# Another order of the units in all sixteen groups of a two-branch attention kernel

## The chip, the cores and the metric

One core of a Trainium2 chip runs the whole program. The metric is the device time of one execution in microseconds; the kernel before takes 842.63 us, the median of three runs from 841.31 to 843.46.

## The reference

The program computes two attentions over the same 2048 x 512 input `x` and mixes them by a gate per row.

```python
g = sigmoid((x * gate_w).sum(-1, keepdims=True))
a = A(x, mem0, Wq, Wk, Wv, Wo)      # recurrent, segment by segment
b = B(x, wq, wk, wv, wo, beta)      # four blocks of 512 rows
return g * a + (1 - g) * b

# A, for each of 64 segments of 32 rows:
h = concatenate([mem, xs])                   # 8 rows of memory, 32 of x
q, k, v = h @ Wq, h @ Wk, h @ Wv             # 32 heads of 128
p = softmax(where(mask, q @ k.T * scale, -1e9))
o = (p @ v) @ Wo
mem = o[:8]; outs.append(o[8:])
```

The eight rows of memory tie the segments together: segment s+1 can project nothing of its memory rows before segment s has ended its output projection. B is softmax attention inside blocks of 512 rows with 32 heads of 16, plus a linear memory that is summed over the earlier blocks.

## The kernel before, in words

**Stages.** First a stage projects the first three blocks of B and turns x (`b_projections`), while the weights of A (Wk, Wq, Wv of 4 MB each) arrive; at about 50 us `plan_a` begins, which is the rest of the program. It walks through 16 groups of four segments. All matrices stay on the chip.

**The recurrent trick.** In a segment, the kernel projects 32 rows: the 8 of memory and the first 24 of the segment. The last 8 rows of the four segments of a group do not depend on the memory for their projection, so they are projected for all four at once, one group ahead, as the *left* units (`KL`, `QL`, `VL`). Their attention output is kept and its output projection is made once a group too (`ol`, then `of`).

**Units.** `plan_a` does not issue its work in a fixed loop. Each piece is a *unit* with a short name, and each group has a list of names (`A_LIST0` to `A_LIST15`, lines 1045 to 1254) that is walked from left to right; a unit issues its instructions when its name comes up. Each engine then runs its instructions in the order in which they were issued, and semaphores hold an instruction until its operands are there. So the lists set the order on every engine and on the DMA queue of SP. `0.` to `3.` ahead of a name is the segment of the group, the digit behind it the half (b) of 16 heads:

- `Q0x`, `Q0y` (and `K`, `V`): the two halves of a projection, eight matmuls of 512 columns each (L1291); small `q0`, `k0`, `v0`: its copy out of PSUM; `TQ0`, `TK0`: the transpose on VectorE (L1303).
- `S`: scores (L1571, L1576); `X`: exponential on ScalarE (L1585); `Y`: mask on VectorE; `M`: sums by matmul (L1606); `L`: logarithm and exponential, the reciprocal of the sums, on ScalarE (L1613, L1616); `N`: normalisation on VectorE (L1620); `n`: the same for the left keys on POOL (L1626).
- `PV` (L1636) and `PL` (L1648): P times V for the segment's keys and for the left ones; `E0a`, ...: their copies out of PSUM; `W0a`, ...: a quarter of the output projection (L1378).
- `H0`, `H1`: the copy of the summed output (tile `WF`); `F0`, `F1`: the *fold*, a matmul that adds four partial sums (L1396); `hm`: the memory for the next segment; `ax`: the finished rows; `xc`, `qt`, `xl`, `oL`: copies on POOL.
- `bS`: scores of two steps of B (L919); `bE`: one exponential of B (L940) and, on a diagonal, the select on POOL (L946); `bP`: P times V of B (L972); `bT`: one of the small works behind it; `pj`, `pp`: projection and copy for the fourth block of B (L823).
- `wl`: issues a load of 512 KB of Wo, eight in all (L549). `VLt`: reloads the left V from DRAM, where the second `VL` copy stored it (L1326, L1334).
- `os`: turns a finished group's rows with one VectorE transpose and stores them with four DMAs (L1453, L1457). `tl`: loads such rows; `tb`, `tbe`, `tf`, `tfe`: the tail that multiplies B's output by its weights, mixes it with A's and stores it.

An `e` at the end of a left, `ol` or tail unit means its second part, mostly the copy out of PSUM. An `i` or a `p` ahead of a left unit belongs to the first or the last group. A name that has nothing to do is passed over.

**The mark `~`.** `A_ENG` says which engine makes a PSUM copy. A `~` behind a name swaps ScalarE and VectorE for that one:

```python
for u in ORDERS[g]:
    v.swap = u[-1] == "~"
    u = u.rstrip("~")
```

**Banks.** PSUM has eight banks. A unit takes its bank when it is issued and gives it back when its copy is issued; where none is free, `relief` issues a pending copy or an exponential of B ahead of its turn in the list. B's scores take two neighbouring pairs.

Of the kernel before, what the change touches and what calls it, by code (L numbers as in the profile page):

```python
# [854 lines left out]
class BAttn:  # L855
# [198 lines left out]
    2.S1 bE bT 2.V0y bE bE 2.X1 2.L0 2.n0 2.Y1 pj 2.v0~ 3.qt pj 2.M1 2.L1 2.N0 2.v1 bP 2.PV0 2.PL0 2.E0b 2.E0a~ pj 2.n1 2.N1 pj 2.PV1 2.PL1 bT pp 2.W0b
    2.E1b 2.W0a 2.E1a 2.W1b pp 2.W1a bP 2.H0 2.H1 bS 2.F0 2.hm0 2.F1 2.hm1~ 2.oL 3.K0x 3.K0y 3.xc 3.k0~ bE 2.ax1 bE bE 3.Q0x 3.Q0y bE 3.TK0 2.ax0~ 3.q0~
    3.Q1x 3.Q1y 3.TQ0 3.q1 3.TQ1 3.K1x 3.K1y 3.k1~ 3.S0 3.X0 3.Y0 3.V0x 3.V1x 3.V0y 3.M0 3.L0 3.n0 bP 3.TK1 3.S1 3.X1 3.V1y 3.v1~ 3.v0 3.N0 bP 3.Y1 3.PV0
    3.PL0 3.E0a~ 3.M1 3.L1 3.n1 pj 3.E0b~ pj 3.W0a 3.N1 3.PV1 pp 3.PL1 3.E1a~ 3.E1b~ 3.W0b 3.W1b 3.oL 3.W1a bS 3.H0 bE 3.F0 3.hm0 3.H1~ 3.ax0 bE 3.F1
# [3 lines left out]
    0.K0x 0.Q0x bE bE 0.Q0y 0.K0y 0.q0~ 0.TQ0 xl 0.k0 0.TK0 0.Q1x 0.K1x 0.Q1y 0.q1 bP bP 0.qt bT 0.K1y 0.k1 0.TK1 0.V1x 0.S0 0.X0 0.TQ1 0.V1y bS VL0x 0.Y0
    VL0 VL0e bE KL1x KL1 KL1e 0.M0 bE bE 0.V0x 0.V0y bE 0.v1~ 0.L0 0.S1 1.qt 0.N0 0.X1 0.Y1 0.n0 QL1x QL1 QL1e pj 0.M1 1.xc 0.v0~ 0.L1 0.n1 bP pj 0.PV0 pp
    0.PL0 0.E0a 0.E0b~ QL0x QL0 0.N1 0.PV1 0.PL1 0.W0b 0.E1a~ 0.W0a 0.W1a 0.E1b 0.W1b 0.H0 QL0e~ 0.H1~ VL1x VL1 0.F0 0.hm0 bP bS 0.xc 1.K1x VL1e 0.F1
    0.hm1~ 0.ax0 1.Q0x bE 1.K0x 1.K0y bE bE 0.ax1 1.k0~ 1.TK0 VLt 1.Q0y bE 1.q0~ 1.TQ0 1.K1y 1.k1 1.TK1 1.Q1x 1.Q1y bP 1.S0 bP 0.oL bS 1.V1x 1.V1y 1.q1
    1.TQ1 1.S1 1.X0 bE 1.V0x 1.Y0 1.M0 bT 1.V0y pj bE bE 1.X1 1.Y1 1.v0 1.M1 bE 1.L0 1.N0 1.n0 1.L1 pj 1.N1 1.v1~ KL0x 1.PV0 1.PL0 1.E0a 2.xc KL0 bP
    1.E0b~ bP 1.PV1 bT 1.n1 pp 1.PL1 1.E1b~ 1.E1a~ 1.W0b 1.oL KL0e~ 1.W0a 1.W1a 1.W1b 1.H0 bS pj 1.F0 1.H1 1.F1 1.hm1~ pj bE 1.hm0 2.K0x 1.ax0~ 2.K0y bE
    bE 2.Q0x 2.Q0y 2.K1x 2.K1y 2.Q1x bE 2.k0 2.TK0 pp bP bP 2.Q1y 1.ax1~ 2.q0~ 2.TQ0 2.q1 2.k1~ bS 2.qt 2.S0 2.V0x ol0x bE 2.TK1 2.X0 2.TQ1 2.Y0 bE 2.S1
    2.X1 2.Y1 2.V0y bE 2.M0 ol0 2.L0 2.n0 bE 2.V1x 2.M1 2.L1 2.n1 2.V1y 2.v0 2.N0 ol1x 2.v1 3.xc 2.PV0 2.PL0 2.E0b 2.N1 ol1 3.qt ol1e~ bP 2.E0a~ 2.PV1
    2.PL1 2.E1b 2.E1a 2.oL 2.W0b 2.W0a 2.W1a bP 2.W1b bS bT pj 2.H0 2.F0 2.H1 2.F1 2.hm1~ pj bE 2.hm0 3.Q0x 3.Q0y bE 2.ax1~ pp 3.K0x 3.K0y bE 3.Q1x 3.Q1y
    2.ax0~ bE 3.q0~ 3.TQ0 3.k0 3.TK0 3.K1x 3.K1y 3.S0 3.k1 bP 3.q1~ 3.V0x 3.TQ1 3.TK1 3.V0y 3.S1 bP 3.X0 3.X1 3.Y0 3.M0 3.L0 3.n0 3.V1x 3.V1y 3.v0 3.Y1  # L1070
    3.M1 3.N0 3.PV0 3.L1 3.n1 3.v1 3.N1 3.PL0 3.E0a 3.PV1 3.PL1 3.W0a 3.E0b 3.W0b 3.E1b 3.W1b 3.E1a~ 3.W1a 3.oL of ofe bS 3.H0 3.F0 3.H1 3.hm0 3.ax0 3.F1
# [4 lines left out]
    bE 0.V1x bT bE bE bE 0.V1y 1.xc 0.S1 0.X1 KL1x VL0x 0.Y1 0.X0 0.Y0 VL0 0.M1 0.M0 QL1x QL1 0.v0~ 0.v1 VL0e 0.L0 0.N0 0.n0 0.L1 0.n1 0.N1 KL1 0.PV0
    0.PL0 0.E0b~ QL1e~ bP bP QL0x 0.E0a 0.PV1 0.PL1 0.W0a 0.E1a~ 0.W0b 0.W1a KL1e~ 0.E1b~ 0.oL 0.W1b 0.H0~ 0.H1~ bS 1.qt bE QL0 0.F0 0.hm0~ 0.F1 VL1x
    0.ax0~ bE 1.K0x 0.hm1~ QL0e~ 1.Q1x 1.Q1y 1.q1~ 1.TQ1 bE bE 1.K0y 1.k0~ 0.ax1 1.Q0x 1.Q0y 1.TK0 1.q0~ 1.K1x 1.K1y bP bP bS 1.k1 1.TQ0 1.TK1 1.V0x 1.S0
    bE bE 1.X0 1.V0y 1.V1x 1.Y0 bE 1.v0 1.S1 2.qt 1.X1 1.Y1 1.V1y 1.v1 1.M0 1.L0 1.N0 1.n0 VL1 1.M1 1.L1 1.n1 KL0x bE 1.N1 1.PV0 1.PL0 1.E0a~ 1.E0b KL0
    KL0e~ 2.xc 1.PV1 1.PL1 1.E1a 1.E1b~ 1.W0b 1.W0a 1.W1a VL1e~ 1.W1b 1.H0 bP 1.H1 bS bP bT 1.F0 1.hm0 1.F1 1.hm1 2.K0x VLt 2.K0y 1.ax1 2.k0~ bE bE 2.Q0x  # L1080
    1.ax0 2.TK0 2.Q0y 2.K1x 2.K1y 2.Q1x 2.Q1y bE 2.q0 2.TQ0 bE 2.k1 2.TK1 1.oL 2.S0 bP bP 2.X0 bS ol0x ol0 bE 2.q1~ 2.TQ1 2.S1 3.qt 2.V0x 2.V0y bE 2.Y0 bE
    2.M0 2.X1 ol1x bE 2.Y1 2.L0 2.n0 2.M1 2.v0 2.L1 2.V1x 2.V1y 2.v1~ 2.n1 2.N0 2.PV0 2.PL0 bP bP 2.N1 ol1 2.E0b~ 2.E0a 2.PV1 2.PL1 2.E1a 2.W0b 2.E1b~
    2.W0a bT 2.W1a ol1e bT 2.W1b 2.H0 bS of 2.F0 bE 2.hm0 3.xc 2.ax0 2.H1~ 2.F1 2.hm1~ 2.ax1~ 3.K0x ofe~ bE 3.Q0x 3.Q0y 3.q0 3.K0y bE 3.k0 3.TK0 3.TQ0 bE
# [776 lines left out]
```

## Time and profile before

| | |
|---|---|
| time, median of 3 runs | 842.63 us (841.31 to 843.46) |
| the profiled execution's own time | 841.9 us |
| its span, first to last instruction | 839.7 us |
| TensorE (PE) busy | 806.0 us, 96% |
| ScalarE (ACT) busy | 590.3 us, 70% |
| VectorE (DVE) busy | 576.5 us, 69% |
| POOL busy | 286.1 us, 34% |
| granted TensorE clock | 1.00 |
| DMA | 57.48 MB, most of it in the first 80 us |

How to read it: busy time of TensorE counts a matmul from its start to its modelled end, and matmuls overlap in the pipeline, so two that follow at once and two with a short gap between can both look busy. The distance from start to start tells more than the busy share. "Idle before" a group is time in which its engine stood, with the engine and line whose work ended that time.

### The profile page before, as it was taken

Reading aid. Unit: us, or ns where it says so; the run is one execution under the profiler, and the core shown is the slowest. Engines: PE = TensorE matmul, PEld = TensorE weight load, DVE = VectorE, ACT = ScalarE, POOL = GpSimd, SP = SyncE. Lnnn points to the kernel's source line nnn. Section 1 sums busy time; section 2 is a strip of 40 time slices with the busy share of each in tenths; the row PEclk is TensorE's granted clock in tenths of the full one; section 3 lists DMA queues with packets and bytes.
Section 4 is the critical chain, followed back from the end, with each engine's and each line's share of the span. In section 5 each row is a group of like instructions: output and inputs, shape, how many; then the busy total and the mean of one; then the engine's idle time right before and its main releaser. Section 6 shows DMA issues by size and latency. Waiting matters only on the chain.

```text
span 839.7 us, 49011 instructions
## 1 busy us (share of the span) xinstructions
PE 806.0 (96%) x21927; PEld 431.3 (51%) x21933; DVE 576.5 (69%) x1395; ACT 590.3 (70%) x1506; POOL 286.1 (34%) x780
## 2 busy tenths in 40 slices
...
PEclk9999999999999999999999999999999999999999
...
GB/s 324 418 360 228 67 45 60 48 31 54 25 30 40 31 44 34 44 38 46 25 44 39 24 56 25 47 38 46 37 19 55 22 55 26 47 35 16 29 41 46
DMA packets 98225, 57.48 MB, mean 68 GB/s; under 512 B 71768, under 2 KB 92128, under 8 KB 96480
## 3 DMA queue, kind: packets, MB, share of 16 engines
...
## 4 chain that ended last, share of the span: by engine, by line
PE 84%; ACT 6%; DMA 4%; DVE 3%; issue 1%; SPq 1%; DVEq 0%; ACTq 0%
PE ps L1291 45%; PE ps L1378 17%; PE ps L1396 3%; PE ps L1636 3%; PE ps L919 2%; PE ps L686 2%; PE ps L972 2%; DMA scr_mzd<-MZ 2%; PE ps L1571 2%; PE ps L1487 1%; PE ps L1606 1%; ACT PT L940 1%; ACT R_sb L1616 1%; ACT WF L390 1%; PE ps L704 1%
## 5 line engine op out<-in xcount | busy, mean ns | idle before, releaser
L946 POOL TENSOR_SCALAR_AFFINE_SELECT PT<-PT 128x128 bf16<-128x128 bf16 (+2 forms) x320 | 118.1, 369 | 202.4 <-ACT PT L940 155.5
L940 ACT ACTIVATE PT<-ps 128x512 bf16<-128x512 f32 x320 | 175.1, 610 | 5.7 <-PE ps L919 4.6
L1291 PE MATMUL ps<-Wv_sb,hT 128*32 128x512 bf16 x2048 | 138.4, 379 | 0.0
L1291 PE MATMUL ps<-Wq_sb,hT 128*32 128x512 bf16 x2048 | 136.7, 379 | 0.7
L1291 PE MATMUL ps<-Wk_sb,hT 128*32 128x512 bf16 x2048 | 135.9, 379 | 1.4 <-ACT PT L940 1.1
L1378 PE MATMUL ps<-Wo_sb,OT_sb 128*32 128x512 bf16 x2048 | 129.2, 380 | 0.7 <-ACT OT_sb L390 0.6
L1626 POOL TENSOR_TENSOR P_sb<-P_sb,R_sb 128x64 bf16<-128x64 bf16 x128 | 51.0, 398 | 135.6 <-ACT R_sb L1616 129.4
L390 ACT ACTIVATE OT_sb<-ps 128x320 bf16<-128x320 f32 x170 | 68.7, 435 | 23.4 <-PE ps L1648 21.9
L1291 PEld LDWEIGHTS ps<-Wk_sb,hT 128*32 128x32 bf16 x2048 | 58.0, 97 | 47.6 <-ACT hT L390 2.1
L1291 PEld LDWEIGHTS ps<-Wq_sb,hT 128*32 128x32 bf16 x2048 | 57.7, 97 | 48.0 <-ACT hT L390 3.6
L390 ACT ACTIVATE WF<-ps 128x256 f32<-128x256 f32 x105 | 35.2, 382 | 55.2 <-PE ps L1378 53.0
L1378 PEld LDWEIGHTS ps<-Wo_sb,OT_sb 128*32 128x32 bf16 x2048 | 47.9, 96 | 45.4 <-ACT OT_sb L390 7.3
L1303 DVE STREAM_TRANSPOSE QT_sb<-QN_sb 128x256 f32<-128x256 f32 x128 | 56.3, 440 | 21.6 <-ACT QN_sb L390 18.0
L390 ACT ACTIVATE QN_sb<-ps 128x512 bf16<-128x512 f32 x78 | 46.9, 604 | 34.3 <-PE ps L1291 32.8
L1303 DVE STREAM_TRANSPOSE KT_sb<-KN_sb 128x256 f32<-128x256 f32 x128 | 56.3, 440 | 20.8 <-ACT KN_sb L390 17.7
L390 ACT ACTIVATE KN_sb<-ps 128x512 bf16<-128x512 f32 x75 | 45.1, 602 | 31.8 <-PE ps L1291 31.1
L1585 ACT ACTIVATE P_sb<-ps 128x224 bf16<-128x224 f32 x128 | 45.9, 360 | 28.4 <-PE ps L1576 20.3
L1291 PEld LDWEIGHTS ps<-Wv_sb,hT 128*32 128x32 bf16 x2048 | 50.1, 95 | 24.3 <-ACT aT_st L390 0.6
L1620 DVE TENSOR_TENSOR P_sb<-P_sb,R_sb 128x160 bf16<-128x160 bf16 x128 | 42.2, 330 | 20.2 <-ACT R_sb L1616 18.2
L392 DVE CAST V_sb<-ps 128x512 bf16<-128x512 f32 x76 | 51.8, 682 | 5.4 <-PE ps L1291 4.8
L392 DVE CAST OT_sb<-ps 128x320 bf16<-128x320 f32 x86 | 41.1, 486 | 19.0 <-PE ps L1648 18.1
L1636 PEld LDWEIGHTS ps<-P_sb,V_sb 32*128 32x128 bf16 x2048 | 23.3, 91 | 59.7 <-DVE P_sb L1620 25.2
...
## 6 DMA issues: line engine op xcount, KB each, us to landing
...
```

What stands on the lines that cost most here:

```text
L390: P.op("act", lambda a: a.activation(dst, src, ACT.Copy), reads=[v.rbank[k] for k in bks], writes=dres, name=name)
L392: P.op("dve", lambda d: d.tensor_copy(dst, src), reads=[v.rbank[k] for k in bks], writes=dres, name=name)
L940: P.op("act", lambda a: a.activation(pt, v.pb[bk], ACT.Exp, scale=v.SCALE_B), reads=[v.rbank[bk]], writes=[rp], name="be%d_%d" % (n, t))
L946: P.op("gp", lambda g: g.affine_select(mv, mv, [[0, len(cut)], [1, 128]], ALU.is_ge, 0.0, base=0, channel_multiplier=-1), reads=[rp], writ ...
L1291: ins = pe.matmul(pb[bk][SEG * j:SEG * (j + 1), :], lhs(c), cols(w, j) if split else w[:, 512 * j:512 * (j + 1)], start=(c == 0), stop=(c ...
L1303: P.op("dve", lambda d: d.transpose(to, src), reads=reads, writes=writes, name=name)
L1378: ins = pe.matmul(pb[bk][SEG * j:SEG * (j + 1), :], lhs(4 * k + j), Wo_sb[:, 4 * k + j, :], start=(first and k == ks[0]), stop=False, skip ...
L1396: ins = pe.matmul(pb[bk][SEG * j:SEG * (j + 1), SEG * n:SEG * (n + 1)], cols, v.fold[:, :], start=True, stop=True, skip_group_check=True)
L1585: P.op("act", lambda a: a.activation(P_sb[:, b, :], pb[bk][:, 0:224], ACT.Exp, scale=SCALE), reads=[rbank[bk]], writes=[Rs("P%d" % b), Rs( ...
L1620: P.op("dve", lambda d: d.tensor_tensor(wide(P_sb, b)[:, :, 0:L], wide(P_sb, b)[:, :, 0:L], R_sb[:, b, :].rearrange("p (i q) -> p i q", q= ...
L1626: P.op(ENG["n"], lambda d: d.tensor_tensor(left(P_sb), left(P_sb), grp04(R_sb[:, b, :]), ALU.mult), reads=[Rs("R%d" % b)], writes=[Rs("P%d ...
L1636: ins = pe.matmul(pb[bks[j]][:, L * i:L * (i + 1)], V_sb[SEG * j:SEG * (j + 1), b, i * E:(i + 1) * E], P_sb[SEG * j:SEG * (j + 1), b, LW * ...
```

## The change

All sixteen lists are replaced by others with the same units. Nothing else of the program differs: the same functions, tiles, engines by default (`A_ENG`) and DMA transfers. In some lists the number of `bE`, `bP`, `bT`, `os`, `tf` and `tfe` differs by one to five, and other lists make up for it. The marks `~` stand at other units, so that 13 PSUM copies in the balance go from VectorE to ScalarE (1506 and 1519 instructions on ScalarE, 1395 and 1382 on VectorE). TensorE has the same instructions in another order, POOL and SP too. The unit `os`, the turn by VectorE, stands at other places: within the first eleven units of a group mostly before, and in groups 8, 13 and 15 some 40 to 50 units in now.

The beginning of the first list, and a stretch of the second half of the last:

```diff
 A_LIST0 = """
-    ixl iKL0x iQL0x iQL0 iQL1x iQL1 iKL0 pj iKL1x iKL0e iKL1 wl 0.Q1x 0.Q1y iQL1e pj 0.K0x 0.K0y 0.q1 0.TQ1 iQL0e~ iKL1e~ bS wl bE iVL0x 0.V0x bE 0.V0y bE
-    0.xc bE 0.Q0x 0.v0~ pp 0.Q0y 0.q0 0.TQ0 bS bP wl bP 0.qt 0.k0~ 0.TK0 pj bE pj wl bE 0.S0 0.X0 iVL0 iVL1x iVL1 0.K1x wl 0.K1y iVL0e~ bE 0.Y0 0.M0 pj xl
-    pp 0.k1 iVL1e wl wl iVLt bE 0.L0 0.TK1 bP wl 0.S1 0.X1 bS 0.Y1 bP bE bE pj bE KL0x 0.M1 0.n0 bE 0.L1 pp 0.V1x 0.V1y 1.xc QL0x 0.v1 QL0 QL0e~ QL1x QL1
-    bP 0.N1 VL0x VL0 0.N0 QL1e~ bT 0.n1 KL1x KL1 VL1x VL0e bP KL0 VL1 KL1e~ 0.PV0 0.PL0 pj VL1e~ 0.E0b~ 0.E0a 0.PV1 0.PL1 0.E1a~ 0.E1b~ KL0e 0.W0a 0.W0b
-    bS pj bE VLt bE bE 0.W1a 0.W1b 0.H0 0.F0 0.oL 0.H1 0.F1 0.hm1~ 1.qt 0.hm0 pp 1.Q1x 1.Q1y 1.Q0x 1.Q0y bE 1.q0 1.TQ0 1.K0x 1.q1 1.TQ1 1.K0y 1.k0 1.TK0
...
+    wl ixl iQL0x iKL0x 0.Q1x 0.Q1y iKL0 iKL0e~ wl iQL0 iQL0e~ 0.Q0x 0.Q0y iQL1x iQL1 0.K0x 0.K0y 0.k0 iQL1e pj 0.q1 wl iKL1x iKL1 iKL1e~ bS bE 0.V0x 0.q0
+    iVL0x 0.TQ0 0.V0y 0.V1x pj 0.V1y iVL0 0.TK0 pj pp 0.v1 bE 0.qt bE iVL0e~ pj bE iVL1x iVL1 xl bS iVL1e bP 0.xc bP QL0x bE bE 0.TQ1 0.v0 0.S0 wl 0.K1x
+    0.K1y KL1x bE wl 0.X0 0.Y0 bE KL1 pj pp 0.k1~ KL1e wl iVLt wl 0.TK1 0.M0 0.L0 QL0 bP wl QL0e bS 0.N0 bP bE VL0x VL0 0.S1 1.qt bE 0.X1 bE QL1x 0.Y1
+    VL0e QL1 pj pp QL1e~ 0.M1 0.L1 KL0x KL0 0.n0 0.n1 VL1x VL1 bE 0.PV0 0.PL0 0.N1 pj 0.E0a 0.E0b~ KL0e 0.PV1 0.PL1 0.E1b~ 0.E1a VL1e~ pj VLt 0.W0b 0.W0a
+    bP 0.W1a bP pp bT 0.W1b 0.H0 0.H1~ 1.xc bS 0.F0 bE 0.hm0 0.ax0 0.F1 0.hm1~ 1.K0x 0.oL bE 1.Q0x 1.K0y 1.k0~ 1.Q1x 1.Q1y 1.q1~ bE 1.TK0 1.Q0y bE 1.K1x
...
 A_LIST15 = """
...
-    2.v0 2.L1 2.n1 tb 2.N1 2.M0 of 2.PV1 2.PL1 2.L0 2.n0 2.E1a ofe 2.N0 2.PV0 2.E1b 2.PL0 2.E0a~ 2.W1a 2.W1b tbe 2.W0a 2.E0b 2.oL 2.W0b 2.H0 2.H1~ os pl0x
-    tf 2.F0 2.hm0 2.ax0 pl0 2.F1 2.hm1 3.K0x 3.Q1x 3.K0y 3.Q0x tfe 3.Q0y 3.K1x 3.K1y 3.k0 tl 3.Q1y 3.TK0 3.q0 3.TQ0 3.k1 3.TK1 pl1x 3.S0 3.V0x 3.q1 3.V0y
...
+    tbe tfe tl 1.E0a 1.E0b 1.PV1 1.n1 1.PL1 1.E1b 2.xc 1.W0a 1.W0b 1.E1a~ 1.oL 1.W1b 1.W1a of ofe os 1.H0 1.H1 1.F0 1.hm0 1.ax0 1.F1 1.hm1 2.qt 1.ax1~
...
+    2.V0x 2.V0y 2.v1 2.Y0 2.n1 2.M0 2.N1 2.PV1 2.v0~ 2.L0 2.PL1 2.E1a 2.E1b tb 2.N0 2.PV0 2.n0 2.PL0 2.E0b 2.W1a tbe tf 2.W1b 2.W0b 2.E0a~ 2.W0a 2.oL pl0x
+    2.H0 2.H1 2.F0 2.hm0 pl0 2.F1 2.hm1 3.K0x tfe 3.Q0x 2.ax0~ 3.Q0y 3.q0~ 3.K0y 3.k0 3.TQ0 3.K1x 3.K1y 3.Q1x tl 3.Q1y 3.TK0 3.S0 3.V0x 3.k1~ 3.q1 3.TK1
...
```

341 lines of the change are left out of this document (170 added, 171 removed).

## The prediction

> **What bounds the kernel now.** First the page: its engine rows, the granted clock, the chain that ended last.
>
> ```profile
> span 839.7 us, 49011 instructions
> PE 806.0 (96%) x21927; PEld 431.3 (51%) x21933; DVE 576.5 (69%) x1395; ACT 590.3 (70%) x1506; POOL 286.1 (34%) x780
> PEclk9999999999999999999999999999999999999999
> PE 84%; ACT 6%; DMA 4%; DVE 3%; issue 1%; SPq 1%; DVEq 0%; ACTq 0%
> ```
>
> TensorE is busy 96% of the span at full clock, but the chain that ended last passes through it for only 84%. The other 16%, some 134 us, is time in which TensorE's next work hung on somebody else, though its pipeline still showed older matmuls as busy. Only that part can move: the change keeps every TensorE operation. Next, where it lies by stage: columns are the window, its length, and busy time (instructions) of PE, weight loads, DVE, ACT, POOL, then clock, DMA share and GB/s.
>
> ```profile
> 54.50:81.30 26.80, 22.45 (x524) 10.37 (x520) 15.45 (x34) 17.56 (x38) 8.38 (x23) 1.00 0.84 262
> 116.80:788.50 671.70, 656.81 (x18788) 353.91 (x18787) 485.15 (x1182) 495.09 (x1290) 238.32 (x610) 1.00 0.16 38
> 788.50:839.70 51.20, 43.76 (x1264) 22.48 (x1264) 30.67 (x75) 24.72 (x67) 7.36 (x19) 1.00 0.17 42
> ```
>
> The first segment (54.5 to 81.3) has TensorE idle for 4.4 us in 27, with the DMA engines 84% busy. Groups 1 to 14 idle only 15 us in 672, the last group 7 in 51. Then the two matmul groups that wait most, P times V (L1636) and the fold (L1396); after the bar stand busy time, mean duration and idle time before them.
>
> ```profile
> L1636 PE MATMUL ps<-P_sb,V_sb 32*128 32x40 bf16 x2048 | 35.5, 177 | 13.4 <-DVE P_sb L1620 7.6 <-ACT OT_sb L390 2.9 <-ACT V_sb L390 0.4
> L1396 PE MATMUL ps<-fold,WF 128*32 128x32 f32 x2048 | 36.9, 199 | 5.3 <-ACT WF L390 2.6 <-ACT hT L390 0.7 <-DVE oTt L996 0.2
> ```
>
> They hold 18.7 us of TensorE's 33.7 idle. A stretch of one segment in the middle, TensorE alone in order of time (start, duration):
>
> ```profile
> 467.37 0.60 PE L1291 MATMUL ps<-Wk_sb,hT 128*32 128x512 bf16 x8
> 467.80 0.60 PE L1291 MATMUL ps<-Wq_sb,hT 128*32 128x512 bf16 x8
> ...
> 471.99 0.28 PE L1606 MATMUL ps<-P_sb,onesb 128*32 128x160 bf16 x8
> 472.09 1.06 PE L1291 MATMUL ps<-Wv_sb,hT 128*32 128x512 bf16 x16
> 473.01 0.28 PE L1606 MATMUL ps<-P_sb,onesb 128*32 128x160 bf16 x8
> 473.12 0.28 PE L972 MATMUL ps<-PT,Vj 128*32 128x128 bf16 x8
> 473.63 0.27 PE L1636 MATMUL ps<-P_sb,V_sb 32*128 32x40 bf16 x16 [0.22 <-DVE P_sb L1620]
> 473.79 0.21 PE L1648 MATMUL ps<-P_sb,VL 32*128 32x64 bf16 x4
> 473.93 0.62 PE L1291 MATMUL ps<-Wv_sb,xL 128*32 128x512 bf16 x8
> 474.55 0.28 PE L1636 MATMUL ps<-P_sb,V_sb 32*128 32x40 bf16 x16
> ```
>
> A unit of eight 512-column matmuls costs 0.43 us (467.37 to 467.80), wherever it stands. After the sums (L1606) ScalarE takes logarithm and exponential, VectorE multiplies, and only then P times V can run: 471.99 to 473.63 and 473.01 to 474.55, so 1.5 to 1.6 us. What the list puts between is the cover; where it is shorter, TensorE stands. So the order of the units is the whole matter.
>
> **The change part by part.** The instructions of TensorE, POOL and the DMA queue are the same in number; sixteen lists are permuted, and the marks that swap a PSUM copy between ScalarE and VectorE are set anew, by which 13 copies go from VectorE to ScalarE.
>
> *Covers outside the first segment.* I counted in both lists, for each segment, the TensorE work (0.43 us per unit as above, the smaller units at their spacing in the same view) that stands between a producer and its consumer, and took as need the shortest distance at which the trace shows no wait: 1.4 us from sums to P times V, 0.63 from the last output projection to the fold, 0.37 from the fold to the next projection, 0.63 from P times V to the output projection, 1.36 from projection to scores, 1.0 from scores to sums. Missing cover, before and after: sums to P times V 21.6 and 20.0 us (47 and 48 places short of 128), output projection to fold 7.5 and 7.7, fold to projection 5.8 and 5.4, P times V to output projection 4.6 and 3.7, projection to scores 2.0 and 1.7, scores to sums 1.8 and 2.0. In all 43.3 and 40.5, so 2.8 us less, 1.05 of it in the first segment, which is costed by itself below: 1.75 us remain, from nine segments that get better by over 0.1 us and seven that get worse. The price of a missing microsecond: the two rows above waited 13.4 + 5.3 = 18.7 us for 21.6 + 7.5 = 29.1 missing, 0.64 each. That is -1.1 us; ends: -1.75 (price 1) and 0 (what the queues of ScalarE and VectorE add hides it).
>
> *The first segment.* Its waits in order:
>
> ```profile
> 56.95 0.40 PE L919 MATMUL ps<-QTj,KTj 32*128 32x256 bf16 x8
> 60.42 0.40 PE L919 MATMUL ps<-QTj,KTj 32*128 32x256 bf16 x8 [0.80 <-DVE QN_sb L392]
> 61.39 0.40 PE L972 MATMUL ps<-PT,Vj 128*32 128x256 bf16 x8 [0.57 <-ACT V_sb L390]
> 66.81 0.29 PE L972 MATMUL ps<-PT,Vj 128*32 128x256 bf16 x4 [1.02 <-POOL PT L946]
> 76.14 0.21 PE L1648 MATMUL ps<-P_sb,VL 32*128 32x64 bf16 x4 [0.90 <-DMA VL<-scr_vld]
> 80.62 0.61 PE L1396 MATMUL ps<-fold,WF 128*32 128x32 f32 x32 [0.55 <-ACT WF L390]
> ```
>
> The first two waits stand behind the second block of B's scores (`bS`). Between the first and second `bS` the old list has five units (`iVL0x 0.V0x 0.V0y 0.Q0x 0.Q0y`, 2.2 us), the new one eleven (4.7 us); the trace needed 3.5 (56.95 to 60.42). Both waits go: -1.4. The one thing that could bring them back is the copy of V, which stood until a store of the stage before had landed:
>
> ```profile
> 57.40 2.07 ACT L940 ACTIVATE PT<-ps 128x512 bf16<-128x512 f32 x4 [0.50 <-PE ps L919]
> 60.74 0.60 ACT L390 ACTIVATE V_sb<-ps 128x512 bf16<-128x512 f32 x1 [1.28 <-DMA scr_mzd<-MZ]
> ```
>
> With the new list the second `bS` comes at about 62, after that copy's 61.4. The third wait (1.02) is for B's four exponentials and POOL's select; ScalarE takes them at 0.52 us each (2.07 for four), and in the old order six other copies stood among them. The new one puts one exponential of A there: 0.33 + 4 x 0.52 + 0.36 + 0.37 of select, about 3.3 with the steps between, against 3.8 of list: -0.8.
>
> ```profile
> L1585 ACT ACTIVATE P_sb<-ps 128x224 bf16<-128x224 f32 x128 | 45.9, 360 | 28.4 <-PE ps L1576 20.3
> L946 POOL TENSOR_SCALAR_AFFINE_SELECT PT<-PT 128x128 bf16<-128x128 bf16 (+2 forms) x320 | 118.1, 369 | 202.4 <-ACT PT L940 155.5
> ```
>
> These rows give the 0.36 and 0.37. The fourth, for the left V's way through DRAM, hangs on SP and the weights of Wo:
>
> ```profile
> 57.63 1.05 SPq L549 DMA_DIRECT2D Wo_sb<-in_A_Wo_dram  x2
> ...
> 65.60 0.43 SPq L1326 DMA_DIRECT2D scr_vld<-VNL  x1
> 66.08 1.57 SPq L549 DMA_DIRECT2D Wo_sb<-in_A_Wo_dram  x2
> 71.68 2.65 SPq L1334 DMA_DIRECT2D VL<-scr_vld  x4
> ```
>
> The new list issues the store some 2.8 us earlier with three loads of 512 KB of Wo ahead instead of five, but TensorE also comes some 4 us earlier. At 262 GB/s (the window above) five to six loads take 10 to 11 us from 57.6; with 4.5 more for the reload (71.68 to 76.14) the data come at 71.7 to 73.5, wanted at 71.7: a wait of 0 to 1.8. I take 0.9, so no gain, and keep 0.9 either way. The fifth loses 0.3, since a `bS` of 0.33 now stands ahead of the fold. First segment: -2.5 us (ends -3.8 and 0).
>
> *Mode switches.* Work on 32-row tiles (P times V, `bS`) after work on 128-row tiles pays something even where nothing waits:
>
> ```profile
> 415.76 1.91 PE L1378 MATMUL ps<-Wo_sb,OT_sb 128*32 128x512 bf16 x32
> 417.60 0.40 PE L919 MATMUL ps<-QTj,KTj 32*128 32x128 bf16 x12
> ```
>
> Four units of 0.43 are 1.73, and the switch came after 1.84: 0.11. Such switches go from 201 to 203: +0.2 us.
>
> The Trainium skill, "TensorEngine Tiling (Array Packing)", section Key Properties, says that changing the tiling mode drains TensorE; the trace agrees, with 0.11 us. By the rule alone, two switches more, the change would be 0.2 us slower, and the sum has it.
>
> *The row turn `os`.* Fifteen times VectorE turns a group's rows, and SP issues four stores.
>
> ```profile
> L1453 DVE STREAM_TRANSPOSE aT_st<-aT_st 128x256 f32<-128x256 f32 x15 | 6.4, 429 | 0.0
> L1303 DVE STREAM_TRANSPOSE KT_sb<-KN_sb 128x256 f32<-128x256 f32 x128 | 56.3, 440 | 20.8 <-ACT KN_sb L390 17.7
> ```
>
> What it delays is the next operation on VectorE. In the old lists that is a copy or a turn of K or Q, on the way to scores, 10 times of 15; in the new ones 9 times, and two stand ahead of `norm` (groups 8 and 13). One fewer is a gain of 0.4 us at most, two in P times V's chain a loss of 0.9 at most; I take 0 and keep both ends. The tail's reload stays a group behind, so the stores cost nothing on SP.
>
> *The 13 copies,* fourteen of Q and K more and some others fewer:
>
> ```profile
> L390 ACT ACTIVATE QN_sb<-ps 128x512 bf16<-128x512 f32 x78 | 46.9, 604 | 34.3 <-PE ps L1291 32.8
> ```
>
> At 604 ns that is 7.8 us more on ScalarE, which is idle for 249 us (839.7 less 590.3): 0, but see the second rival.
>
> *Sum:* -1.1 - 2.5 + 0.2 = -3.4 us. The profiled execution took 841.9 (839.7 and 2.2 around it), which makes 838.5; the median shown is 842.63, 0.7 above it, so I predict 839.2.
>
> **The rivals.** *No change:* the weights set when the first segment ends, since the last piece of Wo must have landed before its last output projection, and TensorE merely waits later. Then -2.5 becomes 0: 842.6 - 1.1 + 0.2 = 841.7. For it: the DMA share of 0.84 there. Against: no output projection waited for Wo before, and Wo's issues now stand earlier.
>
> *Slower, ScalarE as local bound:* summing durations by list, ScalarE has more work than TensorE in 11 segments before (10.4 us over) and in 15 after (14.4 over), the worst being segments 2 and 51 with 2 us. If the surplus lands on P times V's chain, it costs 4.1 us once, or twice, 8.2, when both blocks' logarithms queue behind it. The middle, 6.1, less the first segment's 2.5: 846.2. It decides from the point where a segment's surplus is over what the next segment leaves free (1 to 2 us). Against: segments 29 and 30 of before, 0.8 and 2.3 over by their lists, have these windows, and in the second, the worst of all, TensorE did not idle at all; ScalarE showed 10.3 us of work in 12.7, since its instructions overlap in part.
>
> ```profile
> 419.10:430.60 11.50, 10.39 (x313) 6.03 (x309) 6.65 (x16) 9.17 (x26) 3.87 (x9) 1.00 0.12 31
> 430.60:443.30 12.70, 12.70 (x368) 6.58 (x361) 8.43 (x23) 10.28 (x27) 4.96 (x13) 1.00 0.25 62
> ```
>
> **How the numbers follow.** Forecast 0.50, no change 0.24, slower 0.26. A difference under 0.3% (2.5 us) is about what a measurement cannot tell. The forecast's own range: first segment -3.8 to 0, covers -1.75 to 0, turn -0.4 to 0.9, switches 0.2: 837 to 844. Taking in the slower case, and 3 us below for what the queues of ScalarE and VectorE may give, which a count does not see (they could also take it): 834 to 847.
>
> **What would show it.** Right: the first segment under 25 us instead of 26.8, without the 0.80, 0.57 and 1.02 waits; L1636 idle about 12 to 13 us; groups 1 to 14 within 2 us of before. Wrong: L1636 waiting longer on ScalarE or on POOL's select, or waits for Wo or VL over 2 us in the first segment.

## The result, and the profile after

The changed kernel takes 837.44 us (median of 5 runs, 837.07 to 839.15), the kernel before beside it 842.84: a ratio of 0.9934, 95% interval 0.9916 to 0.9952. A second measurement of the same two programs (`e12_same_again` below) gave 0.9952 (0.9938 to 0.9967). By the ratios the change saves 4 to 5.6 us (by the medians 3.5 and 5.4); the forecast was 3.4. The profiled execution took 837.07, with this page:

```profile
span 835.4 us, 49003 instructions
PE 807.0 (97%) x21933; PEld 434.8 (52%) x21933; DVE 572.8 (69%) x1382; ACT 596.6 (71%) x1519; POOL 284.3 (34%) x780
PEclk9999999999999999999999999999999999999999
PE 83%; ACT 7%; DVE 4%; DMA 2%; issue 2%; SPq 2%; POOL 0%; DVEq 0%; ACTq 0%
```

The work is the same (six matmuls are missing from the trace before), the clock is full, ScalarE has 6.3 us more and VectorE 3.7 less, and the span is 4.3 us shorter. Another half microsecond of the gain lies outside the span: the execution's own time was 841.9 for a span of 839.7, so 2.2 more, and is 837.07 for 835.4, so 1.7 more. Every execution on record shows this, 2.12 to 2.31 us with the kernel before and 1.67 to 1.85 with the new first list. Next the same three stages as before (the first segment, groups 1 to 14, the last group), cut so that each holds the same number of matmuls within one:

```profile
54.37:80.39 26.02, 22.30 (x523) 11.33 (x518) 15.17 (x33) 16.02 (x37) 7.32 (x21) 1.00 0.85 272
115.10:785.60 670.50, 656.58 (x18788) 354.49 (x18785) 482.94 (x1176) 501.31 (x1297) 236.92 (x611) 1.00 0.16 38
785.60:835.40 49.80, 44.10 (x1264) 22.90 (x1264) 29.80 (x72) 24.89 (x70) 7.46 (x19) 1.00 0.17 43
```

The first segment went from 26.80 to 26.02 us only, groups 1 to 14 from 671.70 to 670.50, the last group from 51.20 to 49.80. The groups of matmuls that waited:

```profile
L1396 PE MATMUL ps<-fold,WF 128*32 128x32 f32 x2048 | 37.1, 199 | 6.2 <-ACT WF L390 2.6 <-ACT hT L390 0.8 <-issue 0.8
L1636 PE MATMUL ps<-P_sb,V_sb 32*128 32x40 bf16 x2048 | 35.5, 178 | 10.2 <-DVE P_sb L1620 6.2 <-ACT OT_sb L390 1.0 <-DVE aT_st L392 0.6
```

P times V (L1636) waits 10.2 us instead of 13.4, the fold (L1396) 6.2 instead of 5.3.

**A measure by segment.** Idle time misses what hides behind the modelled ends of matmuls. So I took, for each of the 64 segments, the distance from the start of its first projection to that of the next one, less what its units take at their spacing when nothing waits (0.43 us for eight matmuls of 512 columns, and so on). What is left is lost time. It is worked out from the starts of all recorded matmuls of each trace (21,927 before, 21,933 after); each number is of one execution.

```text
lost us           first   1-3    4-59   60-62   last
before             6.81   5.60  58.86   4.40    2.93
after              6.02   4.80  57.67   4.46    1.42
after, again       6.75   4.79  57.44   4.45    1.42
```

In the first pair the lost time falls by 4.2 us, about all that the span lost. The last column is one segment out of 64, and it holds over a quarter of the gain.

**The last segment.** Of the kernel before, VectorE, then SP, then TensorE, in order of time:

```profile
821.08 0.42 DVE L392 COPY WF<-ps 128x256 f32<-128x256 f32 x1 [1.75 <-ACT WF L390]
821.42 0.43 DVE L1453 STREAM_TRANSPOSE aT_st<-aT_st 128x256 f32<-128x256 f32 x1
...
828.31 0.41 DVE L1620 TENSOR_TENSOR P_sb<-P_sb,R_sb 128x160 bf16<-128x160 bf16 x1
830.48 0.75 DVE L1520 SCALAR_TENSOR_TENSOR aTg<-aTg,g_sb,t_sb 128x512 bf16<-128x512 bf16 x1 [1.76 <-ACT V_sb L390]
831.15 0.32 DVE L1620 TENSOR_TENSOR P_sb<-P_sb,R_sb 128x160 bf16<-128x160 bf16 x1
```

```profile
821.88 3.03 SPq L1457 DMA_DIRECT2D scr_aTd<-aT_st  x4
824.96 0.60 SPq L1522 DMA_DIRECT2D out_dram<-aTg  x1
826.94 0.33 SPq L1476 DMA_DIRECT2D aTg<-scr_aTd  x1
```

```profile
831.61 0.28 PE L1636 MATMUL ps<-P_sb,V_sb 32*128 32x40 bf16 x16 [1.01 <-DVE P_sb L1620]
```

The row turn (L1453) stands on VectorE behind a copy that waits for the last output projection (821.08). Its four stores hold SP for 3.03 us. Behind them comes the store of the tail (L1522), and behind that, because it fills the same tile `aTg`, the reload for the next tail (L1476, 826.94). The tail's last operation (L1520) waits for that reload and starts at 830.48. The last normalisation (L1620) stands behind it at 831.15, and P times V at 831.61. After, VectorE and SP:

```profile
825.28 0.32 DVE L1620 TENSOR_TENSOR P_sb<-P_sb,R_sb 128x160 bf16<-128x160 bf16 x1 [0.29 <-ACT R_sb L1616]
825.94 0.75 DVE L1520 SCALAR_TENSOR_TENSOR aTg<-aTg,g_sb,t_sb 128x512 bf16<-128x512 bf16 x1 [0.34 <-ACT t_sb L1495]
826.61 0.43 DVE L1620 TENSOR_TENSOR P_sb<-P_sb,R_sb 128x160 bf16<-128x160 bf16 x1
```

```profile
808.51 3.65 SPq L1457 DMA_DIRECT2D scr_aTd<-aT_st  x4
...
817.84 0.35 SPq L1522 DMA_DIRECT2D out_dram<-aTg  x1
819.57 0.33 SPq L1476 DMA_DIRECT2D aTg<-scr_aTd  x1
```

The stores go out at 808.5, nine us ahead of the tail's store, and the reload at 819.57, over six us before L1520 starts. The profile names a copy of V as the releaser at 830.48; L1520 doesn't read it, and of its operands the product of B's output had been there since 828.73. The reload took 3.4 us from issue to landing in that trace, so it landed at about 830.3, and I took it for the operand that came last. `e4_turn_early` below tests that.

**The first segment.** TensorE's waits after, and ScalarE between the first two blocks of B's scores:

```profile
57.04 0.40 PE L919 MATMUL ps<-QTj,KTj 32*128 32x256 bf16 x8
63.64 0.40 PE L919 MATMUL ps<-QTj,KTj 32*128 32x256 bf16 x8 [0.90 <-ACT PT L940]
67.89 0.29 PE L972 MATMUL ps<-PT,Vj 128*32 128x256 bf16 x4
75.04 0.21 PE L1648 MATMUL ps<-P_sb,VL 32*128 32x64 bf16 x4 [1.03 <-DMA VL<-scr_vld]
79.68 0.33 PE L1396 MATMUL ps<-fold,WF 128*32 128x32 f32 x16 [0.41 <-ACT WF L390]
```

```profile
57.66 0.59 ACT L940 ACTIVATE PT<-ps 128x512 bf16<-128x512 f32 x1
61.02 0.62 ACT L390 ACTIVATE t_sb<-ps 128x512 bf16<-128x512 f32 x1 [2.77 <-POOL t_sb L841]
61.53 1.08 ACT L940 ACTIVATE PT<-ps 128x512 bf16<-128x512 f32 x2
```

The waits of 0.57 and 1.02 are gone, but the second block (`bS`) came at 63.64, and waited 0.90 where it had waited 0.80. The new list has the copy of the fourth block's projection (`pp`, tile `t_sb`) behind the first exponential; that copy needs POOL to have cleared the tile (L841). The profile names nothing that the clearing waited for, but it started 0.10 us behind the last landing of the four stores of V (`scr_vd`) of the stage before: 60.64 and 60.74 here, 60.27 and 60.37 before. ScalarE stood 2.77 us, with the exponentials behind it that `bS` waits for.

### The profile page after: what moved, and what is told of

It reads as the page before. It is cut to its first block, busy times and chain, and to the rows that moved or that the text cites. A ratio compares the mean times of both kernels' runs of the same rounds, so it can differ in the third digit from the quotient of the medians.

```text
span 835.4 us, 49003 instructions
## 1 busy us (share of the span) xinstructions
PE 807.0 (97%) x21933; PEld 434.8 (52%) x21933; DVE 572.8 (69%) x1382; ACT 596.6 (71%) x1519; POOL 284.3 (34%) x780
## 4 chain that ended last, share of the span: by engine, by line
PE 83%; ACT 7%; DVE 4%; DMA 2%; issue 2%; SPq 2%; POOL 0%; DVEq 0%; ACTq 0%
PE ps L1291 44%; PE ps L1378 16%; PE ps L1396 3%; PE ps L1636 3%; PE ps L686 2%; PE ps L919 2%; PE ps L972 2%; PE ps L1571 1%; PE ps L1487 1%; PE ps L1606 1%; PE ps L704 1%; ACT PT L940 1%; ACT R_sb L1616 1%; ACT WF L390 1%; DVE P_sb L1620 1%
## 5 line engine op out<-in xcount | busy, mean ns | idle before, releaser
L1291 PE MATMUL ps<-Wq_sb,hT 128*32 128x512 bf16 x2048 | 138.4, 379 | 0.6
L390 ACT ACTIVATE OT_sb<-ps 128x320 bf16<-128x320 f32 x167 | 67.0, 434 | 24.3 <-PE ps L1648 22.8
L390 ACT ACTIVATE QN_sb<-ps 128x512 bf16<-128x512 f32 x85 | 50.9, 600 | 29.9 <-PE ps L1291 28.8
L390 ACT ACTIVATE KN_sb<-ps 128x512 bf16<-128x512 f32 x82 | 49.3, 602 | 28.0 <-PE ps L1291 27.4
L1620 DVE TENSOR_TENSOR P_sb<-P_sb,R_sb 128x160 bf16<-128x160 bf16 x128 | 42.5, 333 | 22.4 <-ACT R_sb L1616 21.2
L1636 PEld LDWEIGHTS ps<-P_sb,V_sb 32*128 32x128 bf16 x2048 | 23.0, 91 | 57.6 <-DVE P_sb L1620 21.8
```

The source lines that it names most:

```text
L390: P.op("act", lambda a: a.activation(dst, src, ACT.Copy), reads=[v.rbank[k] for k in bks], writes=dres, name=name)
L1291: ins = pe.matmul(pb[bk][SEG * j:SEG * (j + 1), :], lhs(c), cols(w, j) if split else w[:, 512 * j:512 * (j + 1)], start=(c == 0), stop=(c ...
L1620: P.op("dve", lambda d: d.tensor_tensor(wide(P_sb, b)[:, :, 0:L], wide(P_sb, b)[:, :, 0:L], R_sb[:, b, :].rearrange("p (i q) -> p i q", q= ...
L1636: ins = pe.matmul(pb[bks[j]][:, L * i:L * (i + 1)], V_sb[SEG * j:SEG * (j + 1), b, i * E:(i + 1) * E], P_sb[SEG * j:SEG * (j + 1), b, LW * ...
```

## The experiments

The kernel before ran beside each: 842.41 us (median of 25) beside e1 to e4, 843.01 (22) beside e5 to e8, 842.95 (11) beside e9 to e12. Ratios are to those.

**One list or set of lists at a time.** `e1_list0` is the kernel before with the new first list alone.

```diff
 A_LIST0 = """
-    ixl iKL0x iQL0x iQL0 iQL1x iQL1 iKL0 pj iKL1x iKL0e iKL1 wl 0.Q1x 0.Q1y iQL1e pj 0.K0x 0.K0y 0.q1 0.TQ1 iQL0e~ iKL1e~ bS wl bE iVL0x 0.V0x bE 0.V0y bE
+    wl ixl iQL0x iKL0x 0.Q1x 0.Q1y iKL0 iKL0e~ wl iQL0 iQL0e~ 0.Q0x 0.Q0y iQL1x iQL1 0.K0x 0.K0y 0.k0 iQL1e pj 0.q1 wl iKL1x iKL1 iKL1e~ bS bE 0.V0x 0.q0
...
```

> The kernel before with the new first list alone. Prediction on record: the first segment gives 2.5 us, so about 840.3. Theory from the two traces (the copy of the fourth block's first projection, le0, stands on ScalarE until a store of the stage before has landed, and B's exponentials behind it): only 0.8 us of the first segment and 0.8 more in segments 1 to 3, so about 841.2, and the second bS of the first segment again at 63.6 us.

Measured: 839.71 us, ratio 0.9976 (0.9959 to 0.9993). The second `bS` came late again, at 63.12. Lost: first segment 6.80 (before 6.81, so the 0.8 expected there did not come), segments 1 to 3 4.79 instead of 5.60, the last 2.42 instead of 2.93 although its list is the old one; and 0.5 us less outside the span (1.7).

`e2_lists1to14` is the kernel before with the new lists 1 to 14.

```diff
 A_LIST1 = """
-    0.K0x 0.Q0x bE bE 0.Q0y 0.K0y 0.q0~ 0.TQ0 xl 0.k0 0.TK0 0.Q1x 0.K1x 0.Q1y 0.q1 bP bP 0.qt bT 0.K1y 0.k1 0.TK1 0.V1x 0.S0 0.X0 0.TQ1 0.V1y bS VL0x 0.Y0
+    0.K0x 0.Q0x bE bE 0.Q0y 0.q0 0.TQ0 0.K0y 0.k0 0.Q1x 0.Q1y 0.q1 0.TK0 0.qt 0.TQ1 0.K1x 0.K1y 0.k1 bP bP 0.S0 bT xl KL1x bS 0.X0 0.Y0 0.V0x 0.TK1 KL1
...
```

> The kernel before with the new lists 1 to 14. Prediction on record: missing cover falls a little, about 1 us faster. Theory from the two traces: groups 1 to 14 lose 1.2 us less, most of it one pause of 1.2 us in segment 51 that no cover explains; about 841.5. Counted over these mixed lists the missing cover is 46.8 us instead of 43.3, since the ends of the lists do not fit each other; by the price of 0.64 this alone would be 2.2 us slower, 844.5 to 845.

Measured: 861.0 us, ratio 1.0247 (1.0218 to 1.0275). Its end, the window and TensorE:

```profile
840.00:863.00 23.00, 8.44 (x80) 2.57 (x80) 3.13 (x5) 2.75 (x4) 0.00 (x0) 0.51 0.24 68
```

```profile
844.01 1.90 PE L1487 MATMUL ps<-woB_sb,oTg 128*32 128x512 bf16 x16 [5.47 <-DMA oTg<-scr_oTd]
```

B's last works came one unit (`bT`) late: the new lists 1 to 14 have three `bT` fewer in all, and the new list 15, which this mixture lacks, has one more. (The old lists have two more in the sum over all sixteen, which find nothing to do.) Four tail units (L1487, the first of them shown) then ran one after the other behind everything, each waiting for its reload, at half clock. This run says nothing of the order inside the lists. `e8_lists1to14` puts the missing `bT` into list 15 of that mixture:

```diff
-    0.S0 0.N1 0.X0 0.Y0 0.n1 0.V0y 0.v0~ 1.xc 0.PV1 0.PL1 0.E1a~ 0.M0 ol0x ol0 0.W1a 0.L0 0.n0 0.E1b 0.N0 0.PV0 0.PL0 0.E0b 0.E0a~ 1.qt tfe 0.W1b 0.oL
+    0.S0 0.N1 0.X0 0.Y0 0.n1 0.V0y 0.v0~ 1.xc 0.PV1 0.PL1 0.E1a~ 0.M0 ol0x ol0 0.W1a 0.L0 0.n0 0.E1b 0.N0 0.PV0 0.PL0 0.E0b 0.E0a~ bT 1.qt tfe 0.W1b 0.oL
```

> As the run with the new lists 1 to 14, with one bT put into the old last list, so that the tail's units find B's rows ready and are not left to the end. Prediction on record: about 1 us less lost by covers outside the first segment. Theory from the traces so far: groups 1 to 14 lose 57.5 us by the new lists and 58.2 by the old ones, so 842 against 842.6, not to be told from before; the last segment keeps its wait.

Measured: 843.33 us, ratio 0.9993 (0.9977 to 1.001): fourteen new lists out of sixteen make no difference that this measurement can tell. By lost time of segments 4 to 59, the traces with the old lists have 58.86, 58.35, 57.94 and 57.71 (mean 58.2), the nine with the new ones 57.1 to 58.4 (mean 57.5): 0.7 us. The two sets overlap. Of the time outside the span, e8 shows the new kernel's 1.7 us, as e1 does, though they have no new list in common; what sets it was not tried.

`e3_list15` has the new last list alone.

```diff
 A_LIST15 = """
-    tf 0.Q1x 0.Q1y 0.K1x 0.K1y 0.Q0x 0.Q0y 0.qt os 0.q1 0.K0x 0.TQ1 0.k1 0.TK1 0.q0 0.S1 0.X1 0.K0y 0.k0 0.Y1 0.TQ0 0.V1x 0.TK0 0.V1y 0.M1 0.v1 0.L1 0.V0x
+    0.K1x 0.K1y 0.k1~ 0.TK1 0.Q1x 0.Q1y 0.q1 tf 0.Q0x 0.Q0y 0.K0x 0.TQ1 0.q0~ 0.qt 0.S1 0.X1 0.Y1 0.TQ0 0.K0y 0.V1x 0.k0 0.TK0 0.V1y 0.M1 0.L1 0.V0x 0.S0
...
```

> The kernel before with the new last list alone. Prediction on record: nothing from the last group's turn, about 842.5. Theory from the two traces: the turn of group 14 early in the last group lets its rows be reloaded in time, and the multiplication that waits for them on VectorE no longer holds the normalisation of the last segment: 1.2 to 1.5 us faster, 841.3, and no wait of over 1 us in the last segment.

Measured: 840.98 us, ratio 0.9988 (0.9972 to 1.0004). The last segment lost 1.43 instead of 2.93. The three parts give 2.0, 0.6 and 1.0 us by their ratios, 3.6 together, each with an interval of about 1.4 us to either side. For the whole, 3.6 lies within the second measurement's interval (2.8 to 5.2 us) and below the first one's (4.0 to 7.1).

**The row turn.** `e4_turn_early` changes one thing in the kernel before: in list 15, `os` of group 14 moves from ahead of `pl0x` to behind `2.N0`.

```diff
-    2.v0 2.L1 2.n1 tb 2.N1 2.M0 of 2.PV1 2.PL1 2.L0 2.n0 2.E1a ofe 2.N0 2.PV0 2.E1b 2.PL0 2.E0a~ 2.W1a 2.W1b tbe 2.W0a 2.E0b 2.oL 2.W0b 2.H0 2.H1~ os pl0x
+    2.v0 2.L1 2.n1 tb 2.N1 2.M0 of 2.PV1 2.PL1 2.L0 2.n0 2.E1a ofe 2.N0 os 2.PV0 2.E1b 2.PL0 2.E0a~ 2.W1a 2.W1b tbe 2.W0a 2.E0b 2.oL 2.W0b 2.H0 2.H1~ pl0x
```

> The kernel before with one unit moved: the second os of the last list from ahead of pl0x to behind 2.N0, so that the turn and its four stores go out some 2 to 3 us earlier. If the late reload of these rows is the cause, the wait of 1.2 us before the last segment's second P times V goes: 1.0 to 1.5 us faster, about 841.5. If another part of the new last list is the cause, the wait stays and the time is 842.6.

Measured: 842.08 us, ratio 1.0008 (0.9991 to 1.0026), so the time does not show the gain: the interval leaves room for 0.8 us of it at most. The clock blurs it (last section): seven of the ten executions have a mean clock below 1, ten of the 25 of the kernel before. The three of e4 at full clock have a median of 839.57, the 15 of before 840.97, 1.4 us more; but three are few. VectorE shows the wait itself:

```profile
817.24 0.44 DVE L1453 STREAM_TRANSPOSE aT_st<-aT_st 128x256 f32<-128x256 f32 x1
...
827.30 0.40 DVE L1620 TENSOR_TENSOR P_sb<-P_sb,R_sb 128x160 bf16<-128x160 bf16 x1
827.75 0.75 DVE L1520 SCALAR_TENSOR_TENSOR aTg<-aTg,g_sb,t_sb 128x512 bf16<-128x512 bf16 x1
828.42 0.43 DVE L1620 TENSOR_TENSOR P_sb<-P_sb,R_sb 128x160 bf16<-128x160 bf16 x1
```

With the turn 2.8 us ahead of that segment's fold (820.08) instead of 0.3 behind it, L1520 follows the first normalisation at once, and the last segment loses 1.56 instead of 2.93. So the place of this one unit makes the wait.

Two runs tried to bring the wait back in the changed kernel. `e5_turn_late` moves `os` to ahead of the last but one segment's folding:

```diff
-    tbe tfe tl 1.E0a 1.E0b 1.PV1 1.n1 1.PL1 1.E1b 2.xc 1.W0a 1.W0b 1.E1a~ 1.oL 1.W1b 1.W1a of ofe os 1.H0 1.H1 1.F0 1.hm0 1.ax0 1.F1 1.hm1 2.qt 1.ax1~
+    tbe tfe tl 1.E0a 1.E0b 1.PV1 1.n1 1.PL1 1.E1b 2.xc 1.W0a 1.W0b 1.E1a~ 1.oL 1.W1b 1.W1a of ofe 1.H0 1.H1 1.F0 1.hm0 1.ax0 1.F1 1.hm1 2.qt 1.ax1~
...
-    2.V0x 2.V0y 2.v1 2.Y0 2.n1 2.M0 2.N1 2.PV1 2.v0~ 2.L0 2.PL1 2.E1a 2.E1b tb 2.N0 2.PV0 2.n0 2.PL0 2.E0b 2.W1a tbe tf 2.W1b 2.W0b 2.E0a~ 2.W0a 2.oL pl0x
+    2.V0x 2.V0y 2.v1 2.Y0 2.n1 2.M0 2.N1 2.PV1 2.v0~ 2.L0 2.PL1 2.E1a 2.E1b tb 2.N0 2.PV0 2.n0 2.PL0 2.E0b 2.W1a tbe tf 2.W1b 2.W0b 2.E0a~ 2.W0a 2.oL os pl0x
```

> The changed kernel with one unit moved: the second os of the last list from behind ofe to ahead of pl0x, about where the kernel before has it. If the late reload of group 14's rows made the wait in the last segment, the wait returns: the last segment loses 1.2 to 1.5 us more, about 838.8. If the rest of the new last list matters and not the turn, the time stays at 837.4.

`e11_turn_later` moves it further, behind `2.hm1`:

```diff
-    2.H0 2.H1 2.F0 2.hm0 pl0 2.F1 2.hm1 3.K0x tfe 3.Q0x 2.ax0~ 3.Q0y 3.q0~ 3.K0y 3.k0 3.TQ0 3.K1x 3.K1y 3.Q1x tl 3.Q1y 3.TK0 3.S0 3.V0x 3.k1~ 3.q1 3.TK1
+    2.H0 2.H1 2.F0 2.hm0 pl0 2.F1 2.hm1 os 3.K0x tfe 3.Q0x 2.ax0~ 3.Q0y 3.q0~ 3.K0y 3.k0 3.TQ0 3.K1x 3.K1y 3.Q1x tl 3.Q1y 3.TK0 3.S0 3.V0x 3.k1~ 3.q1 3.TK1
```

> The changed kernel with the last row turn (os of list 15) moved behind 2.hm1, that is behind the fold of the last but one segment, as late after it as before or up to 0.8 us later. e5_turn_late had put it 1.9 us ahead of that fold, 2.2 us earlier than the kernel before has it, and the wait had not come back. Theory (the late turn keeps four stores ahead of the tail's store and reload on SP, and VectorE's fin14 waits for the reload ahead of the last normalisation): fin14 waits again, the last segment loses 2.6 to 4 us instead of 1.4, the wait in front of P times V there is 1.2 to 2.0 us, time 1.2 to 2.5 us over the changed kernel, 838.6 to 840. Rival (other moves of list 15 took the wait away): the last segment loses 1.4 again, time as the changed kernel.

Measured: e5 839.06 us, ratio 0.9946 (0.9927 to 0.9964); e11 839.46, ratio 0.9938 (0.9916 to 0.996). Both lose 1.42 in the last segment: a miss, and mine of the same kind twice. VectorE of e11:

```profile
820.13 0.43 DVE L1453 STREAM_TRANSPOSE aT_st<-aT_st 128x256 f32<-128x256 f32 x1
...
829.65 0.75 DVE L1520 SCALAR_TENSOR_TENSOR aTg<-aTg,g_sb,t_sb 128x512 bf16<-128x512 bf16 x1 [0.34 <-ACT t_sb L1495]
```

I had put the turn behind the fold in the list, but it ran at 820.13, 1.84 us ahead of the fold (821.97). In the kernel before the copy of `WF` ahead of it on VectorE (821.08) waits for the output projection and holds the turn. In the changed list that copy (`2.H1`, without its `~`) is ScalarE's, so VectorE has nothing to wait for and runs the turn as soon as it comes. What both runs show is a turn that is still early enough, 1.84 us ahead of the fold in the changed kernel; 0.3 behind it, in the kernel before, it was too late. Where in between it decides was not tried, and the wait was not brought back in the changed kernel.

**The price of a missing cover.** `e7_less_cover` is the changed kernel with 23 V projection units moved from behind the sums to ahead of them, which takes 7.9 us of cover from between sums and P times V (20.0 missing become 27.9); for instance in list 1:

```diff
-... 2.V1x 2.M1 2.V1y 2.L1 ...
+... 2.V1x 2.V1y 2.M1 2.L1 ...
```

> The changed kernel with 23 projection units (0.43 us each) moved from behind the sums to ahead of them, so that less work stands between sums and P times V in 23 segments; the missing cover there grows from 20.0 to 27.9 us. At the recorded price of 0.64 that is 5.0 us slower, 842.4; at a price of 1, 7.9 us, 845.3. If the cover count has no bearing on the time, 837.4.

Measured: 844.75 us, ratio 1.001 (0.9995 to 1.0025); against the changed kernel's 0.9934 and 0.9952, 5 to 6.5 us slower. Lost time of segments 4 to 59 went from 57.5 to 64.1, 6.6 for 7.9 missing, 0.8 each. P times V in its trace (the line numbers behind the lists are two lower in this kernel):

```profile
L1634 PE MATMUL ps<-P_sb,V_sb 32*128 32x40 bf16 x2048 | 35.8, 178 | 13.9 <-DVE P_sb L1618 7.3 <-ACT OT_sb L390 1.8 <-ACT V_sb L390 0.9
```

Its idle time rose by 3.7 only, so the idle column shows only part of what a missing cover costs.

**What ends the first segment.** `e6_copy_later` is the changed kernel with `pp` behind the exponentials that it held up:

```diff
-    iVL0x 0.TQ0 0.V0y 0.V1x pj 0.V1y iVL0 0.TK0 pj pp 0.v1 bE 0.qt bE iVL0e~ pj bE iVL1x iVL1 xl bS iVL1e bP 0.xc bP QL0x bE bE 0.TQ1 0.v0 0.S0 wl 0.K1x
+    iVL0x 0.TQ0 0.V0y 0.V1x pj 0.V1y iVL0 0.TK0 pj 0.v1 bE 0.qt bE bE pp iVL0e~ pj iVL1x iVL1 xl bS iVL1e bP 0.xc bP QL0x bE bE 0.TQ1 0.v0 0.S0 wl 0.K1x
```

> The changed kernel with the first pp (the copy le0 of the fourth block's projection) behind B's first four exponentials instead of behind one of them. If le0, which stands on ScalarE until a store has landed at about 61 us, is what kept the first segment's gain from coming, the second bS comes at 62.3 to 62.6 us instead of 63.6 and the first segment ends 1.0 to 1.5 us earlier: about 836.2. If the copies of V, which wait for the same store, hold it anyway, nothing changes: 837.4.

Measured: 838.25 us, ratio 0.9936 (0.9915 to 0.9957), not told apart from the changed kernel. The second `bS` did come earlier, without its wait. But the wait moved, and something came with it; TensorE, and the window behind:

```profile
62.89 0.40 PE L919 MATMUL ps<-QTj,KTj 32*128 32x256 bf16 x8
75.32 0.21 PE L1648 MATMUL ps<-P_sb,VL 32*128 32x64 bf16 x4 [2.25 <-DMA VL<-scr_vld]
```

```profile
77.00:81.00 4.00, 4.00 (x64) 1.68 (x52) 1.98 (x5) 1.81 (x5) 0.00 (x0) 0.57 0.35 108
```

TensorE reached the left P times V 0.9 us earlier and waited 2.25 us for the reload of the left V instead of 1.03. Then its clock fell to 0.57 over four us, at the cost of 1.7 us (4 x 0.43). `e9_reload_first` puts the reload `iVLt` ahead of one load of Wo and of `pp`, and `e10_reload_copy` has both edits:

```diff
-    0.K1y KL1x bE wl 0.X0 0.Y0 bE KL1 pj pp 0.k1~ KL1e wl iVLt wl 0.TK1 0.M0 0.L0 QL0 bP wl QL0e bS 0.N0 bP bE VL0x VL0 0.S1 1.qt bE 0.X1 bE QL1x 0.Y1
+    0.K1y KL1x bE wl 0.X0 0.Y0 bE KL1 pj iVLt pp 0.k1~ KL1e wl wl 0.TK1 0.M0 0.L0 QL0 bP wl QL0e bS 0.N0 bP bE VL0x VL0 0.S1 1.qt bE 0.X1 bE QL1x 0.Y1
```

> The changed kernel with one edit in list 0: the reload of the left V (iVLt) stands ahead of the copy pp, and one load of Wo that stood ahead of it stands behind it. In the changed kernel the four reloads were issued from 68.77 on, behind a load of Wo that held SP for 1.02 us, and landed at 75.0, where TensorE had waited 1.03 us. Theory A (the queue ahead of the reload makes that wait): the reloads are issued at about 67.1, land at about 73.5, the wait in front of the left P times V (L1648) goes to under 0.2, and the time is 1.0 to 1.2 us under the changed kernel, about 836.3. Theory B (bandwidth of all transfers together sets the end of the first segment, whatever their order): the wait moves to the output projection of the first segment, which then waits for Wo by 0.5 to 1 us, and the time is that of the changed kernel within 0.4 us. Under A the granted clock is 1.00 over 72 to 84 us as well, since no wait of 1 us is left there.

> The edits of e9_reload_first and e6_copy_later together: TensorE reaches the first P times V about 0.9 us earlier than in the changed kernel (72.8 against 73.7 of its span) and the reload is issued some 1.7 us earlier. Theory A: wait for the reload 0 to 0.6 us instead of 2.25 as with the copy alone, the clock stays at 1.00 between 76 and 84 us (with the copy alone it fell to 0.57 from 77 to 81), the first segment loses some 4.5 to 5 us instead of 6.0, and the time is 835.5 to 836.3. Theory B (the sum of the transfers sets the end): waits for Wo take its place, 837.5 to 838.3 as with the copy alone.

Beside them ran the changed kernel itself:

> The changed kernel unaltered, beside the other three and on the same chip, to tell what differs between two executions of the same code. Expected: ratio 0.993 to 0.995, the first segment loses 6.0 again with the wait for the reload at about 1.0, the last segment 1.4. The 1.1 us pause of TensorE in segment 35 (at 502 us, ahead of which nothing shows) is gone or stands elsewhere if it is chance; it stands in the same place if it belongs to the order of this list.

Measured: e9 839.87 us, ratio 0.9962 (0.9948 to 0.9977); e10 839.75, 0.9955 (0.9941 to 0.997); e12 839.47, 0.9952 (0.9938 to 0.9967). No edit beats the changed kernel. All six executions of e9, five of the six of e10 and four of the six of e12 have a mean clock below 1; at full clock e10 has one of 837.83 and e12 two of 837.77 and 838.62, so there is no gain there either. TensorE of e9, then of e10, then of e12:

```profile
79.25 0.61 PE L1378 MATMUL ps<-Wo_sb,OT_sb 128*32 128x512 bf16 x8 [0.52 <-DMA Wo_sb<-in_A_Wo_dram]
81.16 0.33 PE L1396 MATMUL ps<-fold,WF 128*32 128x32 f32 x16 [0.97 <-ACT WF L390]
```

```profile
74.64 0.27 PE L1636 MATMUL ps<-P_sb,V_sb 32*128 32x40 bf16 x16 [1.20 <-ACT R_sb L1613]
80.80 0.33 PE L1396 MATMUL ps<-fold,WF 128*32 128x32 f32 x16 [1.31 <-ACT WF L390]
```

```profile
76.37 0.21 PE L1648 MATMUL ps<-P_sb,VL 32*128 32x64 bf16 x4 [2.01 <-DMA VL<-scr_vld]
```

In e9 and e10 the wait for the reload is gone, as theory A said. In e9 one for Wo (0.52) and one at the fold (0.97) have come; in e10 a wait behind a logarithm (1.20) and 1.31 at the fold. So theory B holds in its result, but its reason (Wo) accounts for 0.5 us of e9 alone. In all three edits another wait came within a few units of the one removed. Of e12 I had expected 6.0 lost and a wait of 1.0; it lost 6.75 and waited 2.01, with the same code. Lost in the first segment, each in one execution: old list 6.81, 6.49 and 6.91 (before, e3, e4); new list 6.02, 6.75, 6.80, 5.71, 6.17 and 5.99 (after, e12, e1, e5, e7, e11); edited 6.1 (e6, 7.81 less the 1.7 of the clock), 5.62 (e9) and 6.36 (e10). By these means the new list is worth 0.5 us there, and two executions of it differ by more, so it is not told from nothing. Why the fold waits 0.41 us in one and 1.92 in another (e11) was not settled.

## Why the prediction was right, and where it was wrong

The sign and the size came out: 837.44 for 839.2 forecast, and gains of 5.6 and 4.0 us by the two ratios for 3.4. The terms did not. Lost time gives, as means over the executions named above: first segment -0.5, segments 1 to 3 -0.75, 4 to 59 -0.7, 60 to 62 0, the last -1.4; in sum -3.3. About 0.45 more lies outside the span, where the prediction kept 2.2 us for both kernels ("839.7 and 2.2 around it"). That makes 3.8; up to 1.8 us of the measured gain are not located.

- *Covers outside the first segment, -1.1:* right in size. Segments 1 to 62 gave -1.45, half of it in segments 1 to 3; that it came through the covers was not tested place by place. The price of 0.64 looks low: e7 shows 0.6 to 0.8 for each us by its time and 0.8 by its lost time.
- *First segment, -2.5:* wrong, -0.5 by the means. The failing sentence is "With the new list the second `bS` comes at about 62, after that copy's 61.4". I had looked at what the copy of V waits for, not at what the exponentials between the two blocks queue behind: `pp`, moved ahead of them, waits for POOL's clearing until 61.02. It came at 63.64; with `pp` behind them (e6) it came at 62.89 without a wait, and even so the segment did not get shorter, since TensorE then waited for the reload for 2.25 us and the clock fell. The wait for the reload stayed, as I had said; the one at the fold, which was to shrink from 0.55 by 0.3, was 0.41 (after) to 1.92 (e11). The expected length of under 25 us came out as 26.02.
- *Row turn, 0:* wrong, and the miss that paid. "The tail's reload stays a group behind, so the stores cost nothing on SP" fails for the turn of group 14, in the last list. There the next tail follows closely, and the four stores stood ahead of a store and a reload through one tile. I had costed what the turn delays on VectorE and had not followed its stores down SP's queue to the operation that waits at their end. Worth -1.4 in lost time; e4 shows it for the wait and the last segment, its median time does not.
- *Mode switches, +0.2:* not visible among differences of this size. No run separates it.
- *The 13 copies, 0:* nothing speaks against it, and no run separates it. ScalarE has 6.3 us more (7.8 estimated), groups 1 to 14 are a us shorter, and the waits of P times V for ScalarE's `OT_sb` copies went from 2.9 to 1.0.
- *P times V idle 12 to 13 us:* 10.2, since the last segment's 1.01 and more is in it.
- *The rivals:* "no change" came nearer for the first segment (0, where -0.5 was measured), but its reason was not seen: TensorE waited there for Wo by 0.52 us in e9 and 0.18 in e11, and in no other of the nine traces with the new first list. ScalarE as local bound was not seen.

Two misses, -0.5 for -2.5 and -1.4 for 0, cancelled but for 0.6. That was luck: the forecast was right in its sum more than in its reasons.
